# Four channel blocks of K transposed by DMA instead of TensorE, and a G table loaded without its zeros

## The chip, the cores and the metric

The kernel runs on one core of a Trainium2 chip. The metric is the device time of one execution in microseconds (us), the median over several runs. The core has five engines with instruction streams of their own: TensorE (PE in the profile, its weight loads PEld), VectorE (DVE), ScalarE (ACT), GpSimd (POOL) and SyncE (SP). SP computes nothing here; its queue issues nearly all DMA transfers, in order.

## The reference

The function is one layer on a sequence of 2048 positions with 640 channels: a convolution block and a dense block, each with a residual sum. All tensors are bf16.

```python
x = A_q
k_shift = sum(k_pad[:, t:t + S, :] * shift_k[:, ks - 1 - t] for t in range(4))   # causal, 4 taps per channel
kv = k_shift * v
y = irfft(rfft(kv padded to 2S) * rfft(ssm_k padded to 2S))[:S] + kv * ssm_D    # long convolution per channel
h = x + layernorm(x) * y
act = mish(layernorm(h) @ w1 + b1)
out = h + act @ w2                                                              # w1 640x1728, w2 1728x640
```

## The kernel before

**Data.** The 640 channels are five blocks of 128 (block m, or b). The 2048 positions are 128 partitions times 16 positions. Short names stand for the steps:

- d_n0 to d_n4, d_k0 to d_k3, d_v0, d_v1, d_x0 to d_x2, d_g0 to d_g7, d_w1, d_w2, d_t2m: loads of ssm_k (N), K, V, the input, the table G, the weights and another table.
- k1pe / k1ev: TensorE transposes of N (L635) into PSUM, and the copies ("evictions") from PSUM to SBUF on ACT (L428) or DVE (L430).
- ktpe / ktev: the same for K (L590). Each block has two halves, x and y, of eight 128x128 transposes each. ktsh (L601, POOL) then makes a copy of one half that is shifted by one column; it serves the part of the four-tap filter that reaches across the boundary.
- cfpe, coef, wsh (L502, L516): the filter's coefficients, spread into small weight matrices, ten products on POOL.
- kspe / kv: the filter as matmuls (L609, L610) and its product with V, which also empties PSUM (L613, DVE).
- s1k, s1v: the first step of the long Fourier transform, of N and of K times V (L561, L562), with evictions. The last letters of a name give its block and part.
- s2k, s2v: the second step, with table G as weights (L662 for N in 22 groups of six frequencies, L697 for K times V), with evictions.
- sw: DMA transfers that swap neighbouring partitions of the transformed N (L678, L679). p1, p2: the products in the frequency domain (L716, L720), on DVE and POOL.
- i1 (L756, L757) and i2 (L813): the inverse transform. y are its evictions, wb and h the sums, bn, pow, hc the second layer norm.
- trd: DMA transposes of the normalised tiles (L849) for most of the positions; trpe does the first two on TensorE.
- m1pe, hb: the first dense matmul (L910) and Mish on ACT (L915). m2q, m2pe, res: the second dense matmul (L931, L943) and the residual sum (L948). d_out: the stores.

**Buffers.** Large SBUF tiles are used several times. `ra` holds K, later K times V, later a table; `rb` holds V and, before that in its first part, the transposed N of block 2, so d_v0 waits until s1kpe of block 2 has read it. `rn` holds N, later swapped spectra, later w2. `uv` holds the transposed K and the wsh matrices before it holds the spectrum of K times V. `xb` holds the other wsh matrices before part of the input. PSUM is a ring of eight banks of 512 fp32 columns.

**Order.** A list of words such as `ktev1y:a` fixes for each step its engine (t PE, a ACT, v DVE, p POOL, d SP's DMA queue, s ACT's DMA queue) and its place among that engine's steps. `_schedule` turns it into a program with planned durations, by which slots and the order of issue are chosen. On the chip every engine takes its steps in that order, and waits on semaphores where a step needs another's result.

Of the kernel before, what the change touches and what calls it, by code (L numbers as in the profile page):

```python
# [12 lines left out]
BF16 = mybir.dt.bfloat16  # L13
# [3 lines left out]
S = 2048  # L17
D = 640
FF = 1728
FP = 1792  # L20
P = 128
# [5 lines left out]
d_id:s wz:v d_dr:s d_sk:s d_go:d wm:t d_n0:d d_n2:d d_n3:d d_x0:d d_n1:d d_n4:d d_k2:d dcpe:t warm:a dcev:v dq0:v k1pe0y:t k1pe0x:t k1pe2y:t d_k3:d  # L27
k1ev0y:v d_k1:d dq2:v k1pe2x:t k1ev0x:v k1ev2y:v k1ev2x:a s1kpe0_0x:t s1kev0_0x:v d_k0:d s1kpe0_3x:t s1kpe0_1y:t s1kpe0_2x:t s1kpe0_2y:t s1kpe2_2x:t
s1kpe2_3x:t s1kpe2_0y:t s1kev0_3x:a ln1_2:v s1kev0_2y:a s1kev0_2x:a dq1:v cfpe:t kz:p ln1p2:p s1kev2_3x:a dq3:v s1kev2_2x:a ln1_3:v s1kev0_1y:v dq4:v
d_g4:d k1pe3y:t k1ev3y:a coef:a d_v1:d wsh4_0:p ln1p3:p k1pe1x:t d_g3:d d_g2:d k1ev1x:a wsh2_1:p wsh0_0:p wsh4_1:p wsh1_1:p wsh3_1:p wsh2_0:p d_g1:d  # L30
k1pe1y:t k1pe3x:t k1ev1y:v k1pe4y:t k1pe4x:t k1ev3x:v k1ev4x:v s1kpe1_0y:t s1kpe2_2y:t s1kpe1_1y:t wsh1_0:p s1kev2_2y:a s1kpe2_1y:t k1ev4y:v
s1kpe3_0x:t s1kev1_0y:a s1kev2_0y:a s1kpe2_1x:t s1kpe1_1x:t s1kpe0_3y:t s1kev0_3y:a s1kev3_0x:v s1kev1_1x:v s1kpe4_0x:t s1kev4_0x:v s1kpe4_3y:t
s1kev4_3y:a s1kpe4_3x:t s1kpe2_0x:t s1kev2_1x:a s1kpe3_2y:t s1kpe4_2x:t ln1_0:v s1kev4_3x:v s1kev3_2y:v s1kev2_1y:a s1kpe0_1x:t s1kpe2_3y:t
s1kev1_1y:v ktpe2y:t s1kev4_2x:a ktev2y:v ktpe1y:t ktpe3y:t ktpe4y:t ktpe0x:t ktpe4x:t ktev1y:a ln1_1:v d_v0:d ktpe0y:t ktev3y:a s1kev2_0x:v ktev4x:v
ktev4y:v s1kev2_3y:a s1kev0_1x:a ktev0y:a ktpe3x:t ktpe2x:t s1kpe3_3y:t s1kpe3_2x:t s1kev3_3y:v s1kpe4_0y:t s1kpe4_1y:t s1kpe4_1x:t s1kev4_1y:a
s1kev3_2x:a s1kpe3_3x:t s1kpe1_3y:t ktev0x:v s1kpe0_0y:t ktev3x:v kspe3_1y:t s1kpe1_0x:t ktev2x:a s1kev1_3y:a s1kev4_0y:a ktpe1x:t s1kpe3_1y:t d_g0:d
s1kev1_0x:a s1kev0_0y:a s1kev3_1y:a s1kpe3_1x:t ktsh4:p wsh0_1:p s1kev4_1x:v ktsh1:p wsh3_0:p ktsh2:p ktsh0:p ln1p1:p ktsh3:p s1kev3_3x:v kv3_1y:v
s1kpe4_2y:t s1kpe1_2y:t ktev1x:v s1kev4_2y:a s1kev3_1x:v s1kpe1_2x:t d_small:p s1kpe3_0y:t s1kev1_2y:v s1kpe1_3x:t kspe0_1x:t kspe1_1x:t s1kev3_0y:v
# [957 lines left out]
```

## Time and profile before

| What | Value |
|---|---|
| Median of three runs | 221.71 us (221.61 to 222.79) |
| Profiled execution, first to last instruction (its own time; the profile gives no other) | 219.6 us |
| PE busy | 212.6 us, 97% |
| DVE busy | 145.1 us, 66% |
| ACT busy | 133.1 us, 61% |
| POOL busy | 75.6 us, 34% |
| DMA moved | 31.03 MB |

A row of a group reads: line, engine, operation, output <- inputs, shape and count; then total busy us and mean ns; then the idle time before these instructions and what ended it. The rows of 40 slices give the busy share of each slice in tenths, 5.49 us a slice. Matmul durations overlap in time, so their spacing, not their mean duration, says what they cost. The clock granted to TensorE was 1.000 throughout.

### The profile page before, as it was taken

What the parts mean: (1) busy time and instruction counts of PE and PEld (TensorE: products, weight loads), DVE (VectorE), ACT (ScalarE), POOL (GpSimd) and SP (SyncE); (2) the same over time, 40 slices, a digit from 0 to 9 for tenths busy, and PEclk for the clock granted to TensorE, in tenths of its full rate; (3) what the DMA queues carried; (4) which work ended last, traced back from release to release, by engine and by line L of the source; (5) the groups of instructions that cost most, each with busy time, mean ns of one, the idle gap of its engine ahead of it and who ended that gap; (6) DMA issues with size and microseconds to landing.
All of it is one profiled execution on the core that took longest, in us unless ns stands there. A gap on an engine that the chain in (4) does not pass through costs nothing.

```text
span 219.6 us, 6285 instructions
## 1 busy us (share of the span) xinstructions
PE 212.6 (97%) x2611; PEld 157.8 (72%) x2618; DVE 145.1 (66%) x324; ACT 133.1 (61%) x265; POOL 75.6 (34%) x112
## 2 busy tenths in 40 slices
PE   8999999999989999999999999999999999999993
PEld 2899889999879999899876644566554444656672
DVE  0799999999999999989699889883210000213023
ACT  2488899999999999997881178600036475300000
POOL 0079997089844007124883371411000000000000
PEclk9999999999999999999999999999999999999999
DMA  6999993417999906996004401552720000000113
GB/s 213 375 419 414 412 403 130 98 23 174 192 263 285 380 10 217 325 359 105 0 0 64 91 14 45 50 103 60 86 79 19 0 3 0 0 0 3 54 60 125
DMA packets 32876, 31.03 MB, mean 141 GB/s; under 512 B 19024, under 2 KB 29264, under 8 KB 32464
## 3 DMA queue, kind: packets, MB, share of 16 engines
q1 hardware_dynamic: 32384, 30.43, 46.3%
q8 instruction: 20, 0.33, 0.7%
q10 hardware_dynamic: 368, 0.20, 0.4%
q14 instruction: 8, 0.07, 0.1%
q0 software_dynamic: 96, 0.00, 0.0%
HBM read 20.47 MB, written 2.62 MB: 105 GB/s over the span
## 4 chain that ended last, share of the span: by engine, by line
PE 76%; ACT 11%; DVE 5%; issue 3%; SPq 2%; DMA 1%; DVEq 0%; ACTq 0%
PE ps L943 26%; PE ps L910 26%; ACT uk L428 8%; PE ps L813 4%; ACT uv L428 3%; PE ps L756 3%; PE ps L757 3%; PE ps L635 2%; PE ps L561 2%; PE ps L473 2%; PE ps L590 2%; DMA xa<-uk 1%; DVE ra L613 1%; PE ps L931 1%; DVE uv L716 1%
## 5 line engine op out<-in xcount | busy, mean ns | idle before, releaser
L910 PE MATMUL ps<-G 128*128 128x512 bf16 (+1 forms) x319 | 58.5, 336 | 0.3
L943 PE MATMUL ps<-rn,uv 128*128 128x320 bf16 (+2 forms) x415 | 58.5, 299 | 0.1
L915 ACT ACTIVATE uv<-ps,b1s 128x512 bf16<-128x512 f32 (+1 forms) x65 | 35.6, 607 | 36.6 <-PE ps L910 34.8
L943 PEld LDWEIGHTS <-uv 128*128 128x128 bf16 x416 | 39.2, 98 | 18.5 <-issue 1.6
L910 PEld LDWEIGHTS <-G 128*128 128x128 bf16 x325 | 31.1, 98 | 24.0 <-issue 0.9
L428 ACT CAST uk<-ps 128x512 bf16<-128x512 f32 (+1 forms) x91 | 47.2, 703 | 1.9 <-PE ps L562 1.4
L948 DVE TENSOR_TENSOR xb<-ps,xb 128x320 bf16<-128x320 f32 (+2 forms) x12 | 5.6, 488 | 42.6 <-ACT uv L915 24.3
L428 ACT CAST uv<-ps 128x512 bf16<-128x512 f32 (+2 forms) x54 | 28.6, 766 | 0.0
L430 DVE CAST uk<-ps 128x512 bf16<-128x512 f32 (+2 forms) x32 | 20.1, 661 | 0.6 <-ACT uk L428 0.5
L756 PE MATMUL ps<-a,uv 128*128 128x128 bf16 x160 | 18.7, 219 | 0.4 <-DVE uv L716 0.3
L756 PEld LDWEIGHTS <-uv 128*128 128x128 bf16 x160 | 17.8, 114 | 0.9 <-DVE uv L716 0.5
L837 POOL TENSOR_TENSOR r<-ve,mhalf 128x1 f32<-128x1 f32 x16 | 9.7, 613 | 25.0 <-DVE ve L834 24.9
L430 DVE CAST uv<-ps 128x512 bf16<-128x512 f32 (+2 forms) x28 | 17.2, 669 | 0.2 <-ACT uv L428 0.2
L948 DVE TENSOR_TENSOR xa<-ps,xa 128x320 bf16<-128x320 f32 x12 | 5.6, 486 | 14.0 <-PE ps L943 13.9
L613 DVE TENSOR_TENSOR ra<-ps,rb 128x512 bf16<-128x512 f32 x20 | 12.9, 683 | 0.3 <-ACT uv L428 0.3
L720 POOL TENSOR_TENSOR rn<-rn,uv 128x1024 bf16<-128x1024 bf16 x5 | 10.6, 2127 | 7.2 <-PE ps L697 7.2
L697 PE MATMUL ps<-uv,G 128*128 128x64 bf16 (+1 forms) x256 | 12.2, 197 | 0.8 <-ACT uv L428 0.6
L662 PE MATMUL ps<-uk,G 128*128 128x160 bf16 x128 | 12.4, 230 | 0.3 <-ACT uk L428 0.2
L697 PEld LDWEIGHTS <-G 128*128 128x128 bf16 x256 | 10.8, 96 | 1.4 <-issue 1.0
L428 ACT CAST rb<-ps 128x512 bf16<-128x512 f32 (+1 forms) x30 | 11.3, 464 | 0.7 <-PE ps L813 0.4
L561 PE MATMUL ps<-cst,ra 128*64 128x128 bf16 x160 | 10.7, 219 | 0.4
L562 PE MATMUL ps<-cst,ra 128*64 128x128 bf16 x160 | 10.9, 222 | 0.0
(111 smaller groups left out, 375.7 us busy)
## 6 DMA issues: line engine op xcount, KB each, us to landing
G<-tab_g SPq DMA_DIRECT2D x8, 512.0 KB, 14.1
rn<-in_A_ssm_k_dram SPq DMA_DIRECT2D x5, 512.0 KB, 6.3
ra<-in_A_k_dram SPq DMA_DIRECT2D x4, 640.0 KB, 11.4
rb<-in_A_v_dram SPq DMA_DIRECT2D x2, 1280.0 KB, 13.9
G<-in_B_w_dram SPq DMA_DIRECT2D x5, 432.0 KB, 7.3
rn<-in_B_w_dram SPq DMA_DIRECT2D x1, 2080.0 KB, 13.4
rn<-uk SPq DMA_DIRECT2D x8, 256.0 KB, 4.3
rb<-uk SPq DMA_DIRECT2D x8, 256.0 KB, 4.5
```

Source lines behind the costliest of these rows:

```text
L428: nc.scalar.copy(o, i)
L430: nc.vector.tensor_copy(o, i)
L561: nc.tensor.matmul(ps[0:64, k, :], lhs, mc, start=True, stop=True)
L562: nc.tensor.matmul(ps[64:128, k, :], lhs, ms, start=True, stop=True)
L613: nc.vector.tensor_tensor(kv_w[:, m, k:32:2, 8 * h:8 * h + 8, :], ps.rearrange("p (l t d) -> p d t l", l=4, t=8), raw_v[:, 8 * h:8 * h + 8 ...
L662: nc.tensor.matmul(ps[:, o:o + 160], g_v[:, f, :], KA[:, :, f, :], start=True, stop=True)
L697: nc.tensor.matmul(ps[:, fl * n:fl * n + n], g_v[:, f0 + h * kf + fl, :], VX[x][:, :, f0 + h * kf + fl, :], start=True, stop=True)
L756: nc.tensor.matmul(pz[:, k, :], V[c.i][:, dg // 4, :, dg % 4], a12[:, 0, :], start=True, stop=False)
L910: nc.tensor.matmul(ph[:, 0:w], w1[:, dc, fc * P:fc * P + P], lnhT_of(u)[:, dc, 0:w], start=(dc == 0), stop=(dc == NDC - 1))
L915: nc.scalar.activation(hb_of(u)[:, fc, 0:w], rt.tile[:, 0:w], ACT.Mish, bias=b1s[:, fc:fc + 1], scale=1.0)
L943: nc.tensor.matmul(po[:, 0:d1 - d0], hb_of(u)[:, fc, tl * P:(tl + 1) * P], w2[:, fc, d0:d1], start=False, stop=(fc == NFC - 2))
L948: nc.vector.tensor_tensor(x, rt.tile[:, 0:d1 - d0], x, ALU.add)
```

## The change

**K.** For blocks 1 to 4 (`KX`) the transposes on TensorE and their evictions are gone. In their place POOL copies K with its elements reordered into a buffer (kp, eight steps of 1024 elements per partition), and a DMA transpose from SP's queue (kx, eight steps of eight 128x128 blocks) writes the transposed half. Block 0 stays as it was. The buffers lie in xb, hc and the end of N's region in rn; the last four wait until N's transposes have read it.

**Shifted copies.** The two halves now lie side by side, 16 columns behind the start of a row of 272, with column 15 zeroed. The shifted half is read as a window that starts one column earlier, so ktsh is gone. Both wsh matrices of a block now lie in uv, and xb is free of them.

**G.** Three quarters of G are zeros. G is now zeroed on chip (gz: four steps, one on DVE, three on POOL), and only its nonzero blocks are loaded: eight transfers of 32 partitions with pieces of 256 bytes. To keep the pieces together, the four frequencies of a group lie interleaved, so a matmul reads its weights with a step of four elements. The rows that G produces change their order, and the table a12 of the inverse transform is permuted to match. A load of G now serves 64 frequencies, four loads each.

**Order.** All of the order list is new. Among its differences: most s2k steps come before the filter (kspe), the loads of G follow K, the first seven kx stand behind d_v0 and the last behind sw0_1, and d_w2 stands behind trd2 and trd3. Several evictions and products change their engine.

```diff
+k1ev1y:a k1ev0y:v dq1:v k1ev0x:v k1pe1x:t s1kpe0_1x:t s1kpe0_3x:t s1kpe0_3y:t s1kpe0_2x:t k1ev1x:v s1kev0_1x:v s1kpe1_1y:t s1kpe1_2x:t s1kpe1_0x:t
...
+ln1_2:v k1pe4x:t s1kev0_2x:a k1ev3y:a k1ev3x:a s1kev1_0x:a k1ev4y:a coef:a wsh3_0:p wsh0_0:p wsh4_0:p d_k0:d d_k1:d wsh0_1:p wsh1_1:p wsh1_0:p kp1_0:p
+d_k2:d d_k3:d kp3_1:p kp1_1:p kp2_0:p d_g7:d d_g0:d s1kpe1_3x:t s1kpe3_0y:t s1kpe2_2x:t s1kpe1_3y:t k1ev4x:v s1kpe3_2y:t s1kpe2_3y:t s1kpe2_3x:t
...
+s2kpe_8x:t d_v1:d d_v0:d kx1_1:d kx1_0:d kx3_0:d kx2_0:d kx2_1:d s2kpe_9x:t kx3_1:d s2kpe_1y:t kx4_0:d ktev0y:v ktev0x:v s2kev_4y:a s2kev_7x:a
...
+s2kev_19y:a s2kev_16x:a s2kpe_2x:t kspe1_1x:t sw0_1:d kx4_1:d s2kev_13x:a s2kev_2x:a kv1_1x:v kspe1_0x:t kspe1_0y:t kspe1_1y:t s1vpe0_1y:t s1vpe0_3x:t
...
+hb0_1:a hb0_5:a m1pe0_6:t m1pe0_2:t i2pc7:t i2pc6:t i2pc8:t y15b:a y10b:a y8b:a trd2:d hb0_2:a trd3:d d_w2:d m1pe0_11:t y7b:v i2pc12:t i2pc5:t ln1_4:v
...
-    T["g"] = np.moveaxis(G, 4, 6).reshape(128, 128 * 128)
+    full = np.moveaxis(G, 4, 6).transpose(5, 0, 1, 2, 3, 4, 6)
+    T["g"] = np.stack([full[d, :, :, d].reshape(32, 32, 4, 32).swapaxes(2, 3).reshape(32, 128 * 32) for d in range(4)])
...
-    g_v = gt[:].rearrange("p (f q) -> p f q", q=P)
+    g_v = gt[:].rearrange("p (b q f) -> p b f q", q=P, f=4)
...
-    kt_s = [t[:, 0:3072].rearrange("p (g a t) -> p g a t", g=8, a=3) for t in at_uv]
-    wsh = [[x.rearrange("p (l n) -> p l n", l=4) for x in (t[:, 3072:3776], xb[:, 704 * m:704 * m + 704])] for m, t in enumerate(at_uv)]
+    kt_s = [t[:, 0:2176].rearrange("p (g n) -> p g n", n=272) for t in at_uv]
+    wsh = [[t[:, 2176 + 704 * k:2880 + 704 * k].rearrange("p (l n) -> p l n", l=4) for k in range(2)] for t in at_uv]
+    KX = [1, 2, 3, 4]
+    KP = dict(zip([(m, h) for h in (1, 0) for m in KX], [xb[:, 0:1024], xb[:, 1024:2048], xb[:, 2048:3072], hc_t[:, 0:1024], *(rn[:, 4096 + 1024 * i:5120 + 1024 * i] for i in range(6))]))
...
-        return lambda: nc.sync.dma_start(gt[:, i * 2048:(i + 1) * 2048], dram["g"][:, i * 2048:(i + 1) * 2048])
+        d, h = i % 4, i // 4
+        return lambda: nc.sync.dma_start(gt[d:P:4, h * 8192:h * 8192 + 8192].rearrange("p (b q) -> p b q", q=512)[:, :, 128 * d:128 * d + 128], dram["g"][d, :, h * 2048:h * 2048 + 2048].rearrange("p (b q) -> p b q", q=128))
+    c_gz = [OP(f"gz{i}", [("dve", 1.77), ("pool", 3.5)], emit=(lambda e, i=i: (nc.vector if e == "dve" else nc.gpsimd).memset(gt[:, i * 4096:(i + 1) * 4096], 0.0))) for i in range(4)]
...
+        for h in (1, 0):
+            def kpf(e, b=b, h=h):
+                src = raw_k[:, h * 8 * D:(h + 1) * 8 * D].rearrange("p (n k r) -> p k r n", k=2, r=20)[:, :, 4 * b:4 * b + 4, :]
+                o = KP[b, h].rearrange("p (k r n) -> p k r n", k=2, r=4)
...
+            kp = OP(f"kp{b}_{h}", [("pool", 1.3), ("dve", 1.15), ("act", 1.0)], d_k[2 * h:2 * h + 2], emit=kpf)
+            k_free[h].append(kp)
+
+            def kxf(e, b=b, h=h):
+                nc.sync.dma_start_transpose(kt_s[b][:, :, 144 - 128 * h:272 - 128 * h], KP[b, h])
+            kt_done[b, h] = OP(f"kx{b}_{h}", ("dma", 1.55), [kp], emit=kxf, lat=3.2)
...
-                    nc.tensor.matmul(o, t[:, q, h, :], w[:, 0:128], start=True, stop=False)
-                    nc.tensor.matmul(o[:, 0:48], t[:, q, 0 if h else 2, :], w[:, 128:176], start=False, stop=True)
+                    nc.tensor.matmul(o, t[:, q, 144 - 128 * h:272 - 128 * h], w[:, 0:128], start=True, stop=False)
+                    nc.tensor.matmul(o[:, 0:48], t[:, q, 144:272] if h else t[:, q, 15:143], w[:, 128:176], start=False, stop=True)
...
-    d_g = [DMA(f"d_g{i}", 0.525e6, emit_g(i), deps=d_n[:1], prio=0.6, lat=4.9) for i in range(8)]
+    d_g = [DMA(f"d_g{i}", 0.35e6, emit_g(i), deps=d_n[:1] + c_gz[i // 4 * 2:i // 4 * 2 + 2], prio=0.6, lat=4.5) for i in range(8)]
```

182 lines of the change are left out of this document (89 added, 93 removed).

## The prediction

> **What bounds the kernel now.** I read the page from the top: busy totals, then the span in slices.
>
> ```profile
> span 219.6 us, 6285 instructions
> PE 212.6 (97%) x2611; PEld 157.8 (72%) x2618; DVE 145.1 (66%) x324; ACT 133.1 (61%) x265; POOL 75.6 (34%) x112
> DVE  0799999999999999989699889883210000213023
> ACT  2488899999999999997881178600036475300000
> DMA  6999993417999906996004401552720000000113
> ```
>
> PE at 97% says little, because overlapping matmuls are each counted in full. DVE and ACT tell more: both are nearly always busy from about 25 us to about 85 us and idle for long stretches later. Four stretches of the windows view show the change of bound. Its columns are stretch and length, then busy time (instructions) of PE, PEld, DVE, ACT and POOL, clock, DMA share and GB/s.
>
> ```profile
> 5.00:25.00 20.00, 19.88 (x419) 18.13 (x418) 17.65 (x40) 14.56 (x24) 12.51 (x14) 1.00 1.02 403
> 25.00:66.00 41.00, 39.20 (x910) 36.27 (x905) 40.50 (x69) 40.50 (x86) 28.84 (x27) 1.00 0.69 197
> 66.00:87.00 21.00, 20.55 (x365) 19.95 (x362) 20.52 (x32) 21.00 (x45) 6.15 (x7) 1.00 0.65 216
> 87.00:219.60 132.60, 128.94 (x925) 81.95 (x929) 66.33 (x184) 55.55 (x112) 27.62 (x56) 1.00 0.29 71
> ```
>
> From 5 to 25 us the DMA engines are full (1.02) and PE has a queue of work. From 25 to 66 us ACT and DVE each work 40.5 of 41 us: copying PSUM into SBUF sets the pace. From 87 us PE alone is the limit. The chain of waits agrees: in the first stretch it runs through the K transposes (L590), afterwards through ACT.
>
> ```profile
> 18.42 4.60 PE ps L590 x72
> 25.93 1.36 ACT uk L428 x3
> 31.39 2.88 ACT uk L428 x6
> ```
>
> **The change part by part.** The sum is made against the profiled span of 219.6 us. The median of the three runs is 221.71 us, 2.1 us more; I carry these 2.1 us unchanged.
>
> *Evictions of K.* Block 0 keeps its transposes (L590); blocks 1 to 4 lose theirs and the eight evictions behind them. Groups by line give the number of evictions, merged timeline rows their real spacing.
>
> ```profile
> L428 ACT COPY uv<-ps 128x1024 bf16<-128x1024 bf16 x4 | 4.0, 1030 | 0.7 <-PE ps L590 0.7
> L430 DVE COPY uv<-ps 128x1024 bf16<-128x1024 bf16 x6 | 3.9, 680 | 0.0
> 19.60 1.93 ACT L428 COPY uv<-ps 128x1024 bf16<-128x1024 bf16 x2 [0.74 <-PE ps L590]
> 22.32 1.28 DVE L430 COPY uv<-ps 128x1024 bf16<-128x1024 bf16 x2
> 25.93 4.05 ACT L428 CAST uk<-ps 128x512 bf16<-128x512 f32 x8
> 54.89 3.67 DVE L430 CAST uv<-ps 128x512 bf16<-128x512 f32 x6
> 60.52 1.28 DVE L720 TENSOR_TENSOR rn<-rn,uv 128x1024 bf16<-128x1024 bf16 x2
> ```
>
> A 1024 copy costs 1.93/2 = 0.97 us on ACT and 0.64 on DVE; a 512 cast 0.51 on ACT and 0.61 on DVE; a product 0.64 on DVE. ACT loses four K evictions (3.9 us), DVE four of six (2.6); two stay on DVE. The new order also moves work, by counting its words. ACT gains one 1024 copy, two s1v and four s2v casts and loses three s2k casts: +0.97 + 3 x 0.51 = +2.5, net -1.4. DVE loses what ACT gains and takes three s2k casts back: -0.64 - 3 x 0.61 = -2.5. It also gets three products from POOL, +1.9. Its net is -3.2. Evictions can be handed from one engine to the other, so I take the mean of the two, **-2.3 us**. The lower end of the gain is ACT's 1.4 alone.
>
> *Transposes of K on PE.* 64 of the 80 go, 64 x 4.60/72 = 4.1 us. They sit in the DMA-bound stretch and delay the evictions, not the end; 4.1 us is the upper end of the gain if nothing takes their place. Their weight-load time also prices the table read below.
>
> *Reading table G with a step of four elements.* The 384 weight loads of L662 and L697 become strided. The products' loads at L756 already have that step, L590 a step of 40.
>
> ```profile
> L697 PEld LDWEIGHTS <-G 128*128 128x128 bf16 x256 | 10.8, 96 | 1.4 <-issue 1.0 <-DVE uv L430 0.2
> L756 PEld LDWEIGHTS <-uv 128*128 128x128 bf16 x160 | 17.8, 114 | 0.9 <-DVE uv L716 0.5 <-issue 0.3
> L590 PEld LDWEIGHTS <-ra 128*128 128x128 bf16 x80 | 5.2, 147 | 0.2
> 41.63 0.31 PE ps L697 x8
> 76.32 0.06 PE ps L757
> ```
>
> A load grows from 96 to about 114 ns, and such loads keep 55 to 60 ns spacing at L757. For the 128 matmuls of L662 (160 columns) that hides. The 256 of L697 now come every 0.31/8 = 39 ns: between 0 and 256 x (57 - 39) = +4.6 us. L590's 51 ns longer load costs only 64 - 55 = 9 ns of spacing, so a load 18 ns longer should cost about 3: 0.8 us of PE time. It lies where ACT and DVE work 40.5 of 41 us: taken as 0. Without that cover it is 0.8.
>
> *Zeros and the load of G.* One quarter of G is zeroed on DVE, three on POOL. DVE waits 5.2 us for its first input and POOL 10.2 us.
>
> ```profile
> DVE d_col L488 <- PE ps L486: 5.2, 1, 5.2
> POOL ve L791 <- DVE mv L787: 10.2, 1, 10.2
> 13.28 1.37 POOL L516 TENSOR_TENSOR uv<-cst,coef 128x704 bf16<-128x704 bf16 x1 [0.78 <-ACT coef L428]
> L467 DVE MEMSET hc<- 128x64 uint32 x1 | 0.1, 112 | 0.8 <-PEq L980 0.8
> L601 POOL COPY uv<-uv 128x1016 bf16<-128x1016 bf16 x5 | 5.1, 1029 | 0.0
> ```
>
> On DVE 2048 words at 112/64 ns or less are at most 3.6 us: hidden. On POOL, 4096 elements at the copy's 1.0 ns are 4.1 us, so three end near 13 us, where the first coefficient product starts now (13.28): 0, and 4 us later at worst for POOL. G shrinks from 4.2 to 1.05 MB in 256-byte pieces; the swap transfers (L678), mostly short packets, show the rate of such pieces.
>
> ```profile
> G<-tab_g SPq DMA_DIRECT2D x8, 512.0 KB, 14.1
> DMA packets 7103, 2.08 MB, mean 189 GB/s; under 512 B 6077, under 2 KB 7101, under 8 KB 7101
> ```
>
> N, x0, K and V are 8.5 MB at the 403 GB/s above, 21 us; G at 189 GB/s takes 5.5 us instead of 10.4. Counted from 2.5 us the loads end near 29 us; in the page's DMA row they fill the engines to slice 5, 33 us. That opens room for the transposes and shortens nothing by itself: 0.
>
> *K's new route.* Eight permutes on POOL (taken at 1.3 us, between the 1.03 of the copy and 2.13 of a two-input product) replace five shift copies; eight DMA transposes follow on SP's queue.
>
> ```profile
> L516 POOL TENSOR_TENSOR xb<-cst,coef 128x704 bf16<-128x704 bf16 x5 | 6.8, 1366 | 0.0
> L720 POOL TENSOR_TENSOR rn<-rn,uv 128x1024 bf16<-128x1024 bf16 x5 | 10.6, 2127 | 7.2 <-PE ps L697 7.2
> L786 DVE BATCH_NORM_STATS2 st<-x 128x6 f32<-128x320 bf16 x8 | 3.5, 482 | 0.7 <-DMA x<-in_A_q_dram 0.7
> G<-hc SPq DMA_TRANSPOSE x14, 2.7
> 121.94 1.21 SPq L849 DMA_TRANSPOSE G<-hc  x1
> ```
>
> Coefficients near 16 us (13.3 now; in the new order more evictions stand before them), six wsh products (8.2), eight permutes and small work put the last permute near 36 us on POOL. On SP the transposes stand behind d_v0, which waits until PE has read block 2 of N: 38 s1k casts at some 0.56 us, ten copies of N at some 0.8 and the statistics' 3.5 are 33 us on two engines from about 8 us, so about 25 to 26 us. A transpose here has 8 blocks against 5 at L849: 8/5 x 1.21 = 1.9 us spacing. Seven are issued by 40 us and landed by 43; sw0_1 and the last follow, landed near 47. Meanwhile PE and the eviction engines have 36 of 43 s2k pieces (18 us of casts, 9 us on two engines) and block 0: kspe1 is wanted near 37 us, kspe2 near 44, kspe4 near 50. Their transposes land near 31, 39 and 47. Cost 0, with 3 to 6 us of margin; past that each microsecond is exposed. The end of the margin is reached at a spacing near 3 us.
>
> The Trainium skill, "VectorE: DVE Perf Modes", section on the three transpose paths, speaks against this: it lists 1309 ns for a 128x128 block through the DMA against 390 ns on TensorE and advises TensorE where PSUM will do. By that figure, an estimate, a transpose of 8 blocks would be 10.5 us and the sum some 50 us worse. The trace disagrees: 5 blocks land 2.7 us after issue, so the page's figure cannot be a rate.
>
> *The rest.* The shift copy's removal frees 5.1 us of POOL, off the path. Past 66 us PE does the same matmuls. One order change matters: w2's load moves behind the transposes trd2 and trd3.
>
> ```profile
> 98.33 17.66 SPq L849 DMA_TRANSPOSE G<-hc  x3
> rn<-in_B_w_dram SPq DMA_DIRECT2D x1, 2080.0 KB, 13.4
> 110.11 0.38 PE ps L931 x4
> 87.73 0.39 SPq L769 DMA_DIRECT2D rn<-in_B_w_dram  x1
> ```
>
> It used to go out at 87.7. Now it goes about 98.3 - 2.3 + 2 x 1.2 = 98.4. Its first reader (L931, m2q0) comes at 110.1 - 2.3 + two 256-wide groups moved ahead of it (1.1) = 108.9. The 13.4 us to landing included other loads' backlog; at 403 GB/s and 2 us it would be 7.6. So it lands between 106.0 and 111.8: between 0 and 2.9 us of stall. I take 0.
>
> **Sum**: -2.3 in evictions, the rest covered: 219.6 - 2.3 = 217.3 us of span, 219.4 us as a median.
>
> **The rivals.**
> 1. *Transposes late (slower).* If SP lets one land before the next starts, the spacing is 8/5 x 2.7 = 4.3 us. kx2 and kx3 then end at 26 + 6 x 4.3 = 52 where they are wanted at 44 to 46; some 2 us of s2v work remain to fill in. 6 us are exposed: 219.4 + 6 = 225.4. For it speaks that traffic of V and the swaps surrounds them; against it, the 1.21 us spacing at L849. It decides above about 4 us of spacing, where the exposed time exceeds the 2.3 gained.
> 2. *POOL late (slower).* Permutes at 2.13 and zeros at 5.7 us each (1.4 ns per element): 5 + 8 x 0.83 = 12 us later, kspe2 near 51, exposed 5: 224.4. Against it: the plain copy's 1.03.
> 3. *w2 late (same).* Stall 2.9 at L931: 219.4 + 2.9 = 222.3.
> 4. *No relief (same).* ACT is relieved by 1.4 only, and strided loads cost 0.8 on PE: 221.1.
> 5. *All of PE's 4.1 us gained (faster).* If the L590 row of the chain is what delays the evictions: 217.6.
>
> **How the numbers follow.** Half a per cent, 1.1 us, is what a measurement of this kernel tells from no change. Chances: forecast 0.45, rival 5 0.16, rival 4 0.08, rival 3 0.09, rival 1 0.15, rival 2 0.07. The forecast and rival 5 are faster, 0.61; rivals 3 and 4 same, some of 3 slower: 0.13; slower 0.26. The range goes from 217.0 to 224.4, leaving out rival 1's tail; the forecast's own is 218.0 to 220.4 (gains of 1.4 to 3.7).
>
> **What would show it.** Right: sixteen matmuls on L590; ACT and DVE full until about 2 us earlier; no PE wait on the transposed tile (uv) or on w2 (rn); the first product on POOL near 13 to 17 us; transposes about 2 us apart. Wrong: PE waits for uv longer than 1 us between 35 and 52 us, or SP holding a transpose behind d_v0 past 30 us; L697's loads far above 114 ns; or ACT and DVE idle in that stretch while G or V is on its way.

## The result and the profile after

The changed kernel takes 227.55 us (median; 227.36 to 229.41) where the kernel before takes 221.76: a ratio of 1.027, 95% interval 1.024 to 1.031. It is slower by 5.8 us; the forecast was 2.3 us faster. The profiled span grew by 6.0 us, from 219.6 to 225.6. Here and below, ratios leave out an execution that is over 1.5% above the fastest of its kernel, while medians keep it.

The page of the changed kernel, its busy totals and the span in 40 slices of 5.64 us:

```profile
span 225.6 us, 6184 instructions
PE 212.0 (94%) x2554; PEld 156.3 (69%) x2554; DVE 146.6 (65%) x325; ACT 128.7 (57%) x255; POOL 97.9 (43%) x122
...
DVE  3789896974999999998979899868200210101141
ACT  2599997983999999899760054750453025420000
POOL 9939999987494600624884565223000000000000
PEclk9999999997999999999999999999999999999999
```

Counted from 1, POOL is busy without a break from slice 4 to slice 8, where it had idle time before; ACT and DVE have holes in slices 7, 9 and 10, and the clock dips in slice 10. The windows view gives the stages (stretch, length, busy time of PE, PEld, DVE, ACT, POOL with instruction counts, clock, DMA share, GB/s):

```profile
5.00:25.00 20.00, 18.89 (x422) 16.33 (x421) 17.27 (x39) 15.96 (x29) 15.97 (x9) 1.00 1.00 335
25.00:66.00 41.00, 34.23 (x749) 32.05 (x747) 33.57 (x56) 34.09 (x72) 35.25 (x37) 0.96 0.93 191
```

Most of the loss lies between 25 and 66 us. ACT and DVE were busy there for 40.5 of 41 us each; now they are busy for 34. PE idles 41 - 34.2 = 6.8 us instead of 41 - 39.2 = 1.8, that is 5.0 us more. The chain of waits names the place (start, length, what; engine, tile and line):

```profile
23.17 2.24 POOL rn L610
25.41 4.51 POOL xb L610 x2
29.91 6.75 POOL rn L610 x3
...
36.72 0.21 POOL uv L532 x5
36.92 2.22 POOL xb L610
39.14 2.25 POOL hc L610
...
42.74 3.98 POOL uv L518 x3
...
48.34 5.64 DMA uv<-hc
...
54.03 0.22 PE ps L624
```

L610 are the permutes (kp), L532 the zeroing of column 15 (kz), L518 the wsh products, L615 the DMA transposes (kx), L623 and L624 the filter's matmuls. Where ACT stood in the chain before, POOL stands now. The groups by line give the prices of a zeroing step (L545) and of a permute (L610, the four that write to rn):

```profile
L545 POOL MEMSET G<- 128x4096 bf16 x3 | 10.4, 3512 | 0.3 <-POOLq L996 0.3
L610 POOL COPY rn<-ra 128x1024 bf16<-128x1024 bf16 x4 | 9.1, 2304 | 0.0
```

A permute takes 2.30 us. Eight of them end at 41.4 us instead of near 36. What waits for them, by the view of waits between 25 and 66 us (engine, tile, line, releaser: us, times, longest):

```profile
PE ps L624 <- DMA uv<-hc: 2.6, 1, 2.6
PE ps L624 <- POOL uv L532: 1.5, 1, 1.5
PE ps L623 <- POOL uv L518: 1.2, 1, 1.2
...
DVE ra L627 <- POOL rn L610: 2.1, 1, 2.1
```

Four different things stand behind the permutes: the last transposes, the zeroed column, the remaining wsh products, and the product kv (L627, DVE), which writes into `ra` and so must wait until the permutes have read K there. SP's queue shows how the last transpose comes so late:

```profile
31.52 5.54 SPq L615 DMA_TRANSPOSE uv<-rn  x3
...
46.93 0.65 SPq L694 DMA_DIRECT2D rn<-uk  x1
47.62 0.66 SPq L695 DMA_DIRECT2D rn<-uk  x1
48.34 1.77 SPq L615 DMA_TRANSPOSE uv<-hc  x1
```

Its permute ends at 41.4 us, but in the queue it stands behind the two transfers of the swap sw0_1, which could not go before 46.9 us; it is issued at 48.3 and PE goes on at 54.0. The swap itself was held by a transpose, by the waits of SP's queue:

```profile
SPq L694 <- DMA uv<-rn: 3.2, 1, 3.2
```

The swap writes into `rn`, where four of the permuted pieces of K lie until their transposes have read them. So the new route also delays the swaps. The stretch in which PE waits, in windows of one microsecond:

```profile
52.00:53.00 1.00, 0.00 (x0) 0.00 (x0) 0.00 (x0) 0.64 (x2) 0.00 (x0) 1.00 0.26 51
53.00:54.00 1.00, 0.00 (x0) 0.00 (x0) 0.00 (x0) 0.00 (x0) 0.86 (x1) 0.76 1.29 278
54.00:55.00 1.00, 0.97 (x16) 0.98 (x17) 0.20 (x1) 0.00 (x0) 1.00 (x1) 0.50 1.35 217
55.00:56.00 1.00, 1.00 (x20) 1.00 (x18) 0.75 (x2) 0.00 (x0) 1.00 (x2) 0.50 1.35 218
56.00:57.00 1.00, 1.00 (x18) 1.00 (x16) 0.61 (x2) 0.83 (x2) 1.00 (x1) 0.54 1.35 217
57.00:58.00 1.00, 1.00 (x37) 0.93 (x36) 1.00 (x2) 0.66 (x2) 0.83 (x3) 1.00 1.35 220
```

While PE waits, its granted clock falls to a half, and it stays there until 57 us: 16 to 20 matmuls per microsecond, and 37 in the next (not all of the same size). At 0.50, 0.50 and 0.54 the lost clock is 0.50 + 0.50 + 0.46 = 1.46 us, an estimate of what it costs.

### The profile page after: what moved, and what is told of

Same layout as the page of the kernel before. It is cut to its first block, busy times and chain, and to the rows that moved or that the text cites. A ratio compares the mean times of both kernels' runs of the same rounds, so it can differ in the third digit from the quotient of the medians.

```text
span 225.6 us, 6184 instructions
## 1 busy us (share of the span) xinstructions
PE 212.0 (94%) x2554; PEld 156.3 (69%) x2554; DVE 146.6 (65%) x325; ACT 128.7 (57%) x255; POOL 97.9 (43%) x122
## 4 chain that ended last, share of the span: by engine, by line
PE 54%; POOL 19%; ACT 10%; DVE 8%; issue 4%; DMA 3%; POOLq 0%; ACTq 0%; DVEq 0%
PE ps L959 19%; PE ps L926 17%; ACT uv L430 6%; POOL uv L518 5%; PE ps L772 4%; POOL rn L610 4%; PE ps L773 4%; POOL xb L610 3%; ACT rb L430 3%; DMA uv<-hc 3%; PE ps L475 2%; POOL ra L818 2%; PE ps L649 2%; DVE st L802 2%; POOL r L808 2%
## 5 line engine op out<-in xcount | busy, mean ns | idle before, releaser
L430 ACT CAST uk<-ps 128x512 bf16<-128x512 f32 (+1 forms) x88 | 44.3, 661 | 3.0 <-PE ps L678 1.5
L430 ACT CAST uv<-ps 128x512 bf16<-128x512 f32 (+2 forms) x60 | 30.0, 672 | 4.9 <-PE ps L713 3.5
L432 DVE CAST uk<-ps 128x512 bf16<-128x512 f32 (+1 forms) x35 | 21.6, 668 | 0.9 <-issue 0.5
L627 DVE TENSOR_TENSOR ra<-ps,rb 128x512 bf16<-128x512 f32 x20 | 12.6, 685 | 6.7 <-PE ps L624 3.4
L518 POOL TENSOR_TENSOR uv<-cst,coef 128x704 bf16<-128x704 bf16 x10 | 13.4, 1368 | 4.0 <-ACT coef L430 4.0
L713 PE MATMUL ps<-uv,G 128*128 128x64 bf16 (+1 forms) x256 | 13.2, 204 | 1.0 <-DVE uv L432 0.8
L432 DVE CAST uv<-ps 128x512 bf16<-128x512 f32 (+2 forms) x22 | 13.3, 666 | 0.4 <-ACT uv L430 0.2
L713 PEld LDWEIGHTS <-G 128*128 128x128 bf16 x256 | 11.7, 116 | 1.7 <-DVE uv L432 0.9
L624 PE MATMUL ps<-uv 128*128 128x48 bf16 x80 | 8.7, 194 | 4.2 <-DMA uv<-hc 2.6
L816 ACT ACTIVATE ra<-xb,nmr,r 128x640 bf16<-128x640 bf16 x4 | 3.6, 916 | 15.9 <-POOL nmr L809 15.9
L732 DVE TENSOR_TENSOR uv<-uv,uk 128x1024 bf16<-128x1024 bf16 (+1 forms) x15 | 10.9, 755 | 0.6 <-POOL rn L736 0.6
L678 PE MATMUL ps<-uk,G 128*128 128x160 bf16 x128 | 10.8, 232 | 0.5 <-ACT uk L430 0.4
```

What stands on the lines that cost most here:

```text
L430: nc.scalar.copy(o, i)
L432: nc.vector.tensor_copy(o, i)
L518: (nc.gpsimd if e == "pool" else nc.vector).tensor_tensor(out, a, b, ALU.mult)
L627: nc.vector.tensor_tensor(kv_w[:, m, k:32:2, 8 * h:8 * h + 8, :], ps.rearrange("p (l t d) -> p d t l", l=4, t=8), raw_v[:, 8 * h:8 * h + 8 ...
L713: nc.tensor.matmul(ps[:, fl * n:fl * n + n], g_v[:, (f0 + h * kf + fl) // 4, (f0 + h * kf + fl) % 4, :], VX[x][:, :, f0 + h * kf + fl, :], ...
L732: eng.tensor_tensor(v, v, K[c.i][:, b0:b1, f0:f1, :], ALU.mult)
```

## The experiments

The theory after the first comparison (P): the permutes are the cause, at 2.30 instead of 1.3 us. The rivals: the order of queues around them (Q), the other parts of the change, and a forecast gain that was never there. Times stand beside 221.7 to 221.9 us of the kernel before, run on the same chip. The changed kernel's 227.55 us comes from its own four runs alone, so experiments are compared with it through the kernel before.

### The price of a permute

**e1: the same copies, read contiguously.**

```diff
-src = raw_k[:, h * 8 * D:(h + 1) * 8 * D].rearrange("p (n k r) -> p k r n", k=2, r=20)[:, :, 4 * b:4 * b + 4, :]
-o = KP[b, h].rearrange("p (k r n) -> p k r n", k=2, r=4)
+src = raw_k[:, h * 8 * D + 1024 * b:h * 8 * D + 1024 * b + 1024]
+o = KP[b, h]
```

> The changed kernel, but the eight permutes on POOL read 1024 neighbouring elements of K instead of elements 40 apart; the filter then works on the wrong elements of K, so this part of the layer is not computed, while every other step keeps its size. Theory P (the permutes' 2.30 us each, against 1.0 us for a plain copy, delay everything that stands behind them on POOL): a permute falls to 1.0 to 1.1 us, the last one ends about 10 us sooner, PE's idle time between 25 and 66 us falls from 6.8 to about 2 us, the clock stays at 1.0, and the time falls to 218 to 221 us. Theory Q (SP's queue: the transposes themselves, and the last one behind a swap transfer): the last transpose still lands near 52 to 54 us, and the time stays within 1.5 us of 227.5. Theory S (POOL is slow because DVE and POOL disturb each other): permutes stay above 1.8 us.

Measured 223.41 us, ratio 1.007 (1.004 to 1.010): 4.1 us of the 5.8 are gone. That is between the two ranges: theory P's 218 to 221 was too low, theory Q's 226 to 229 too high, and S fell. One group of e1:

```profile
L610 POOL COPY rn<-ra 128x1024 bf16<-128x1024 bf16 x4 | 4.0, 1033 | 0.0
```

and the stage by windows:

```profile
25.00:66.00 41.00, 36.79 (x835) 34.65 (x830) 37.06 (x63) 38.02 (x81) 27.33 (x37) 1.00 1.12 217
```

So the same number of elements, written to the same places, costs 1.03 us read in a row and 2.30 us read with a step of 40 elements (80 bytes). PE's idle time falls from 6.8 to 4.2 us, not to the 2 that P expected, and the clock stays whole in this profiled execution. In four of e1's ten executions the mean granted clock was 0.991 or 0.992, like the 0.992 of the changed kernel's profiled execution. The six at 0.997 or above took 221.69 to 224.48 us, these four 223.19 to 226.22. And the kernel is still not faster than before.

**e7: the loops exchanged**, four neighbours read, written with a step of 128.

```diff
-src = raw_k[:, h * 8 * D:(h + 1) * 8 * D].rearrange("p (n k r) -> p k r n", k=2, r=20)[:, :, 4 * b:4 * b + 4, :]
-o = KP[b, h].rearrange("p (k r n) -> p k r n", k=2, r=4)
+src = raw_k[:, h * 8 * D:(h + 1) * 8 * D].rearrange("p (n k r) -> p k n r", k=2, r=20)[:, :, :, 4 * b:4 * b + 4]
+o = KP[b, h].rearrange("p (k r n) -> p k n r", k=2, r=4)
```

> The changed kernel with the permutes' two inner loops exchanged: four neighbouring elements are read, and written 128 elements apart. Same bytes, same result. If POOL's time follows the step of what it reads, a permute falls to 1.0 to 1.5 us and the time to 222 to 225 us. If it follows the number of access-pattern dimensions or any step that isn't one, a permute stays at 2.2 to 3 us and the time at 227 us or above.

Measured 244.87 us, ratio 1.104, from two executions. Both expectations for the permute fell:

```profile
L610 POOL COPY rn<-ra 128x1024 bf16<-128x1024 bf16 x4 | 19.0, 4973 | 0.0
```

Reading runs of four and writing with a step costs 5.0 us, more than reading with a step and writing in a row. Which of the two makes it, the short runs or the step of the writes, this run doesn't tell. Either way this reordering of 1024 elements on POOL costs two to five times a copy.

**e6: the permutes shared out**, four on POOL, two each on ACT and DVE, with kz first and the last transpose ahead of the swap.

```diff
-d_k2:d d_k3:d kp3_1:p kp1_1:p kp2_0:p d_g7:d
+d_k2:d d_k3:d kp2_0:p d_g7:d
...
-s1kev3_3x:a kp3_0:p
+s1kev3_3x:a kp3_1:a kp3_0:p
...
-kz:p s1kpe3_1x:t kp2_1:p kp4_1:p s1kev3_1x:a s1kev4_2y:v s1kev4_0x:a
+s1kpe3_1x:t s1kev3_1x:a s1kev4_2y:v kp1_1:v s1kev4_0x:a
...
-s1kev2_0y:a ln1_0:v
+s1kev2_0y:a kp2_1:a ln1_0:v
...
-ln1_1:v s1kev0_0y:v
+ln1_1:v kp4_1:v s1kev0_0y:v
```

> The changed kernel with four of the eight permutes on ACT and DVE (two each), the other four on POOL, and kz and the last transpose ahead. All of the layer is computed. Theory P: POOL's chain is 9.2 us shorter, less the wait for coefficients nothing is added there, the last permute ends near 33 us; two permutes on ACT and DVE cost these engines about 1 to 1.5 us each, that is 2 to 3 us per engine in a stretch where they have idle time: 221 to 224 us. Theory Q (rate of the transposes): 224 to 226 us. Below 220.5 us it would beat the kernel before.

Measured 226.69 us, 1.023 (1.020 to 1.025), above both ranges. The same permute on ACT and DVE:

```profile
L608 ACT COPY xb<-ra 128x1024 bf16<-128x1024 bf16 x2 | 4.7, 2334 | 0.9 <-DMA ra<-in_A_k_dram 0.9
L610 DVE COPY xb<-ra 128x1024 bf16<-128x1024 bf16 x1 | 2.0, 2020 | 0.6 <-DMA ra<-in_A_k_dram 0.6
```

They cost 2.33 and 2.0 us there (the second one on DVE 1.7), on the engines that set the pace; besides, they wait for K in front of evictions that PE needs. The windows show what follows:

```profile
20.00:22.00 2.00, 0.00 (x0) 0.00 (x0) 2.00 (x2) 2.00 (x1) 2.00 (x2) 1.00 0.49 98
...
28.00:32.00 4.00, 4.00 (x65) 3.66 (x63) 2.36 (x4) 3.34 (x7) 4.00 (x2) 0.50 0.37 89
```

PE idles some 2.9 us from 20 us on, and its clock is at a half until about 32.5 us.

### The rest of the change, alone

**e8: the table G alone** on the kernel before (zeroed on chip, loaded without its zeros, read with a step; K as before). **e3: G and the windows** instead of shifted copies, all five blocks on TensorE.

```diff
-nc.tensor.matmul(ps[:, o:o + 160], g_v[:, f, :], KA[:, :, f, :], start=True, stop=True)
+nc.tensor.matmul(ps[:, o:o + 160], g_v[:, f // 4, f % 4, :], KA[:, :, f, :], start=True, stop=True)
...
-nc.gpsimd.tensor_copy(t[:, :, 2, 1:128], t[:, :, 1, 0:127])
```

> The kernel before with only table G loaded without its zeros. The pair of parts (table and windows) was slower by 0.33%. If the table makes that (strided weight loads: 384 loads of 113 ns against 96), the time is again 222.2 to 222.8 us. If the windows make it (a window that starts 30 bytes into a row), the table alone stays within 0.15% of the kernel before, 221.4 to 222.0 us.

> The kernel before with two of the change's three parts: table G loaded without its zeros (four zeroing steps, weights read with a step of four elements) and the shifted copies of K replaced by windows. All five blocks of K stay on TensorE. Theory P and theory Q both hold that these parts cost nothing: 220.5 to 222.5 us. Theory G (the strided weight loads, 113 ns against 96, and the short packets cost time): 223.5 us or more.

Measured 222.11 us (1.002, 1.000 to 1.003) for e8 and 222.64 (1.003, 1.002 to 1.005) for e3: 0.3 us, and 0.7 (by the ratio) to 0.95 (by the medians) with both. e8 lies between its two ranges, e3 just above its first; whether table or windows cost more is not settled. The larger group of weight loads in e3:

```profile
L698 PEld LDWEIGHTS <-G 128*128 128x128 bf16 x256 | 11.7, 115 | 1.1 <-issue 0.7
```

It grew from 96 ns to 115, where 114 was forecast, and the whole table costs 0.3 us. These parts don't explain the loss.

### The queues and the clock

**e2: kz ahead of everything on POOL, the last transpose ahead of the swap.**

```diff
-gz1:p gz3:p dcev:v
+gz1:p gz3:p kz:p dcev:v
...
-kz:p s1kpe3_1x:t kp2_1:p
+s1kpe3_1x:t kp2_1:p
...
-sw0_1:d kx4_1:d
+kx4_1:d sw0_1:d
```

> The changed kernel with two words of the order moved: the zeroed columns of the shifted window (kz) go ahead of the permutes on POOL, and the last transpose goes ahead of the first swap transfer on SP. Theory Q: the two waits that these words cause (1.5 us for the zeroed column, up to 2.8 us for the last transpose) go, and with them part of the clock loss: 223 to 225 us. Theory P: the last permute still ends at 41 us and the products for blocks 2 and 4 still stand behind it, so that waits for those take their place: 225.5 to 227.5 us.

**e4: PE kept busy** while it waits, with twelve matmuls on zeros before the first kspe4 step.

```diff
-p2_0_3:p p2_0_2:p kspe4_0x:t
+p2_0_3:p p2_0_2:p fill:t kspe4_0x:t
+for _ in range(12):
+    nc.tensor.matmul(ps[:, 0:512], wz, wz4, start=True, stop=True)
```

> The changed kernel with twelve matmuls on zeros (some 2.6 us) put on PE just ahead of the filter of block 4, where PE idles. If the granted clock falls because PE is idle, it stays at 1.0 from 54 to 58 us, and the time falls by 1 to 1.5 us, to about 226.2. If the clock does not follow PE's idling, or its fall is covered, the time stays at 227.5 us, or rises by up to 1 us where the matmuls delay the filter.

e2 measured 226.51 us (225.99 without one execution of 230.39), 1.019 (1.014 to 1.024): in P's range, and these two words of the order are worth 1.0 to 1.6 us. The waits for the column and for the last transpose are gone, but PE waits for casts of DVE instead,

```profile
PE ps L565 <- DVE uv L432: 2.2, 2, 2.1
```

and the clock falls to 0.50 behind that wait. e4 measured 226.10, 1.019 (1.016 to 1.021), 1.45 us less than the changed kernel, and the clock no longer falls in its windows:

```profile
52.00:53.00 1.00, 1.00 (x6) 0.49 (x5) 0.10 (x1) 0.82 (x2) 0.00 (x0) 1.00 0.44 23
...
54.00:56.00 2.00, 1.57 (x40) 1.41 (x39) 0.86 (x2) 0.06 (x1) 2.00 (x2) 1.00 1.33 233
```

The mean clock was 0.999 or 1.000 in all four executions of e4 and 0.983 to 0.992 in all four of the changed kernel. Work that computes nothing makes the kernel faster: the fall of the clock follows the idling of PE, and its price agrees with the 1.46 us estimated above. The Trainium skill, "TensorE: Matmul & The Clock Gate", Part 1, states two levels, full and a half, and a fall after an idle window of about 3.4 us. The levels agree with the 1.00 and 0.50 here; the length doesn't, as a wait of 2.6 us was enough in the changed kernel.

**e5: e1 and e2 together.** **e11: e5 with five DVE products (p1, p2) moved behind the casts.** **e12: e2 with the same move.**

```diff
-s1vpe4_0x:t p1_0_3:v p2_0_7:v p1_0_2:v s1vev2_3x:a
+s1vpe4_0x:t s1vev2_3x:a
...
-s1vpe2_1x:t p2_0_6:v s1vev2_1y:a
+s1vpe2_1x:t s1vev2_1y:a
-s1vev2_0x:a p2_0_1:v s1vev4_2y:v
+s1vev2_0x:a s1vev4_2y:v
...
-s1vev3_1x:v s1vev3_2y:v
+s1vev3_1x:v s1vev3_2y:v p1_0_3:v p2_0_7:v p1_0_2:v p2_0_6:v p2_0_1:v
```

> Both edits together: the permutes read neighbouring elements (so the filter works on the wrong elements of K), and kz and the last transpose go ahead. If the permutes' length and the last transpose's place behind the swap are separate causes, the 2.0 us wait for the last transpose that the first alone still had goes too: 220.5 to 222 us, the level of the kernel before. If the transposes' own rate on the queue is what is left (three took 9.5 us there), the time stays at 222.5 to 224.

> The kernel of both edits (permutes that read neighbouring elements, so that the filter works on the wrong elements of K; kz and the last transpose ahead) with five DVE products (p1_0_3, p2_0_7, p1_0_2, p2_0_6, p2_0_1) moved behind the casts of s1v. There PE waited 2.0 us for casts behind these products, and the clock fell to 0.50 for 7 us. If that wait and the clock were what kept it at 224.4 us, the clock stays at 1.0 and the time is 220 to 222 us. If the rest is elsewhere, 223 to 225 us.

> The changed kernel with kz and the last transpose ahead and the same five products moved behind the casts; the permutes keep their 2.30 us and all of the layer is computed. Theory P: what remains is the permutes' delay, about 4 us over the kernel with cheap permutes: 224 to 226 us. If the order behind the permutes was the larger cause, 221 to 223 us.

Measured 224.40 us (1.012, 1.010 to 1.014), 227.07 (1.022, 1.018 to 1.026) and 228.33 (1.027, 1.024 to 1.030). All three lie above both of their ranges. In e5 PE no longer waits for a transpose; a DVE product that took 2.60 us at 53.2 stood ahead of casts instead, by its waits

```profile
PE ps L565 <- DVE uv L432: 2.0, 1, 2.0
```

and the clock fell later, and for longer (to 65 us):

```profile
57.00:58.00 1.00, 0.00 (x0) 0.00 (x0) 1.00 (x3) 1.00 (x3) 1.00 (x1) 1.00 0.90 226
...
59.00:62.00 3.00, 3.00 (x53) 2.68 (x53) 3.00 (x6) 1.07 (x2) 3.00 (x3) 0.50 1.03 231
```

Moving those products away turned the wait into another one (L713 waiting 3.3 us for a cast of DVE, in e11 and e12 alike). Orders mended by hand at one place opened a gap at the next; e1's 223.41 stayed the best of these. e1's profiled execution waited 1.9 us for its last transpose without a fall of the clock, e5's 2.0 us with one, and e1's own executions differ in their clock. What decides it was not settled.

### Fewer blocks

**e9: block 4 alone, e10: blocks 2 and 4**, by the new route in the order of before (K's other blocks on TensorE, windows, table G as before).

```diff
-wsh2_0:p d_g1:d
+wsh2_0:p kp4_1:p kp4_0:p d_g1:d
...
-d_g7:d d_g5:d
+d_g7:d d_g5:d kx4_1:d kx4_0:d
...
+KX = [4]
```

> The kernel before, its order, table and nine of ten transposed pieces as they were, with the new route for block 4 of K alone (two permutes on POOL in the place of the shift copies, two DMA transposes on SP's idle stretch near 25 us) and the windows in place of all shift copies. Theory P (the route costs nothing as long as POOL has room): two permutes of 2.3 us replace five shift copies of 1.03, PE loses 16 transposes (1.0 us) and DVE two evictions (1.2 us): 220.6 to 221.7 us. If the route costs in itself (transposes beside V's load, a wait for a DMA instead of a copy), 222.5 us or more.

> The same with blocks 2 and 4 on the new route: four permutes, 9.2 us on POOL against 5.1 for the shift copies, which must end before the first product of K and V can overwrite K (26.5 us in the kernel before). Theory P: POOL's chain is 4 us longer than in the kernel before, the first products wait, and the time lies at 221 to 223.5 us, above that of one block. If POOL had room for four, it is below the one-block kernel: 220 to 221 us.

Measured 222.92 us (1.004, 1.003 to 1.006) and 227.77 (1.026, 1.023 to 1.028). e9 went against theory P: one block, with room on POOL, is 1.0 us slower, the case in which the route costs in itself (the windows, which e9 has too, can be part of it). e10 lies 4 us above its range: two blocks in this order cost as much as four in the new one. e10's waits:

```profile
DVE ra L631 <- POOL xb L605: 4.4, 2, 3.0
...
PE ps L627 <- POOL uv L518: 3.1, 1, 3.1
```

Here the products that overwrite K come early, and they wait 4.4 us for the permutes: the dependency through `ra`. PE waits 3.1 us for a wsh product that stands behind the permutes.

### The route taken apart

Cheap permutes and better orders all ended above the kernel before. So was the forecast gain there at all, and what does each half of the route cost? Four runs answer it.

e13, plain loads in the place of the transposes and no permutes (e14 keeps the eight kp):

```diff
-d_k2:d d_k3:d kp3_1:p kp1_1:p kp2_0:p d_g7:d
+d_k2:d d_k3:d d_g7:d
...
-nc.sync.dma_start_transpose(kt_s[b][:, :, 144 - 128 * h:272 - 128 * h], KP[b, h])
+nc.sync.dma_start(kt_s[b][:, :, 144 - 128 * h:272 - 128 * h], A_k.rearrange("b (p a) d -> p (b a d)", a=NT)[:, h * 5120 + 1024 * b:h * 5120 + 1024 * b + 1024].rearrange("p (g n) -> p g n", n=128))
```

e15, transposes of one contiguous copy (e16 has the last of them ahead of the swap, as e2):

```diff
+if b == KX[0]:
+    kp = OP("kp1_0", [("pool", 1.3)], d_k[0:2], emit=lambda e: nc.gpsimd.tensor_copy(KP[1, 1], raw_k[:, 0:1024]))
...
-nc.sync.dma_start_transpose(kt_s[b][:, :, 144 - 128 * h:272 - 128 * h], KP[b, h])
+nc.sync.dma_start_transpose(kt_s[b][:, :, 144 - 128 * h:272 - 128 * h], KP[1, 1])
```

> The eight permutes are left out, and the eight DMA transposes become plain loads of 256 KB of K from DRAM at the same places of the queue; the transposed K is not formed, so the filter works on other elements. This keeps everything else of the change: evictions and TensorE transposes gone, table G read with a step, the new order. If the forecast's relief of 2.3 us is there once K's route costs nothing: about 219.5 us (218.5 to 220.5) beside 221.7 of the kernel before. If table and windows cost the 0.9 us that they cost alone and the order hides the rest of the relief: 221 to 222. If something besides the route of K slows the changed kernel: above 223.5.

> As e13, but with the eight permutes back on POOL, at 2.3 us each; their results are used by nothing, while the product that overwrites K still waits for them. If the permutes delay through POOL alone (the zeroed column, the filter's weights and the overwriting of K queue behind them): 3 us or more above e13, about 225 to 226.5. If they delay through the transposes that wait for them: within 1 us of e13, and the difference to the changed kernel's 227.5 lies in the transposes.

> The changed kernel with its eight DMA transposes, but with one contiguous copy of 1024 elements of K on POOL instead of the eight permutes; all eight transposes read that one copy, so the filter works on other elements. It completes the four combinations: neither (e13, 220.2), permutes alone (e14, 224.0), transposes alone (this one), both (the changed kernel, 227.5). If the transposes cost little by themselves and only their lateness behind the slow permutes counts: within 1 us of e13, about 220 to 221. If they hold up the queue and the other transfers by themselves, and the two costs add: 3 us above e13, about 223 to 224.

> As e15, with the last transpose ahead of the swap sw0_1 in SP's queue instead of behind it. If what e15 costs above e13 is the last transpose held behind the swap: within 0.7 us of e13. If the transposes' own transfers cost it: no better than e15.

| | no permutes | eight permutes |
|---|---|---|
| plain loads | e13: 220.19 us, 0.992 (0.988 to 0.995) | e14: 223.97 us, 1.009 (1.005 to 1.012) |
| DMA transposes | e15: 221.86 us, 0.999 (0.996 to 1.001) | changed kernel: 227.55 us, 1.027 (1.024 to 1.031) |

e16 measured 221.45 us, 0.997 (0.994 to 1.001). The stage from 25 to 66 us in e13, by windows:

```profile
25.00:66.00 41.00, 38.98 (x870) 36.72 (x869) 39.90 (x67) 40.49 (x86) 22.31 (x25) 1.00 0.95 241
```

in e14:

```profile
25.00:66.00 41.00, 37.13 (x833) 34.77 (x834) 38.04 (x63) 38.39 (x80) 38.78 (x38) 1.00 0.88 226
```

and in e15:

```profile
25.00:66.00 41.00, 37.94 (x856) 35.66 (x851) 38.40 (x65) 39.30 (x84) 21.60 (x24) 1.00 1.08 224
```

e13 lies in the range of the forecast's relief. e14 is more than 3 us above e13, the case of a delay through POOL alone, though it is 1 us below the time named for it. e15 and e16 lie between their ranges. With the route out of the way ACT and DVE are full again, PE idles 2.0 us, and the kernel is 1.6 us faster than before (the traffic of the plain loads is in that time). The permutes alone, whose results nobody reads, cost 223.97 - 220.19 = 3.8 us: through POOL's queue and the overwriting of K, with no transpose behind them. e14's waits name the same three (zeroed column, wsh product, K), beside one of 1.2 us on PE for which the profile shows no releaser:

```profile
PE ps L623 <- POOL uv L518: 1.2, 1, 1.2
...
PE ps L624 <- POOL uv L532: 0.6, 1, 0.6
...
DVE ra L627 <- POOL rn L610: 1.2, 1, 1.2
```

The transposes alone, in the place of plain loads, cost 1.7 us. The place behind the swap is some 0.4 of that (e16), which the overlapping intervals don't tell from nothing, and PE waits 1.2 us for a transpose in both. In SP's queue of e15 (start, length) they wait for no permute:

```profile
24.66 17.80 SPq L608 DMA_TRANSPOSE uv<-xb  x7
```

Seven take 17.80 us, 2.54 each on average, but single ones 1.3 to 5.2. That is not a price of the transposes alone: e13's seven plain loads take 13.38 us at the same place of the queue, right behind the loads of G and V, and in the changed kernel, where they are issued later, a transpose takes 1.2 to 1.8 us.

Both costs together make 220.19 + 3.8 + 1.7 = 225.7; the changed kernel takes 227.55. The missing 1.9 us exist only where both meet. The clock stays at 1.00 in this stage in the profiled executions of e13, e14 and e15 and falls in the changed kernel's, where the longest wait is 2.6 us and e4's gain was 1.45 us. (By the mean clock, one of e14's four executions, three of e15's ten and all four of the changed kernel had such a fall.) Of the four, only the changed kernel has a swap that waits for late transposes out of `rn`, too; how the 1.9 us divide is not shown.

No version that computes the whole layer beat the kernel before; the nearest is e8 at 222.11 us.

## Why the prediction was wrong

**The step that failed** is "Cost 0, with 3 to 6 us of margin" for "K's new route", and first in it the price of the permutes: "taken at 1.3 us, between the 1.03 of the copy and 2.13 of a two-input product". Neither row bounds it. Both are operations that read runs of neighbouring elements; the permute reads with a step of 40 elements, and costs 2.30 us, above both ends. The rows had a warning: weight loads with that same step (L590) took 147 ns against 96. The Trainium skill, "GPSIMD Engine Reference", section on performance pitfalls, states for custom code on POOL that reads with a step above 8 bytes cost half as much again; if that held for the built-in copy, 1.03 would become 1.5 us, an estimate. The direction agrees with the trace, the size doesn't: 2.30 / 1.03 = 2.2.

The price is not the whole of it. With permutes at 1.03 us, below the 1.3 taken, e1 still takes 223.41 us, 4.0 above the forecast; with one such copy in the place of eight, e15 takes 221.86, 2.5 above it; e13, without permutes or transposes, is 0.8 above it. The margin was not there even at the price assumed.

**The second failure is who waits.** The step "kspe1 is wanted near 37 us, kspe2 near 44, kspe4 near 50" counted only the readers of the transposed K. The permutes also hold kv, which overwrites K in `ra` (2.1 us of waiting, and 4.4 in e10), the zeroed column, which stands behind six of them in POOL's list (1.5), and the last wsh products (1.2). The working named none of these, but each can be read from the order list and the buffers. e7, where a permute takes 5.0 us, makes it plain: there PE waits 16.2 us for the zeroed column. e14 shows that the permutes cost 3.8 us with no transpose behind them, so a margin counted for the transposes alone did not cover this path.

**Point by point.**
- Evictions, -2.3 us: e13, all of the change but the route's permutes and transposes, gives -1.6 us (220.19, in the range of 218.0 to 220.4 stated for the forecast). No run has the evictions alone.
- TensorE's 4.1 us from the K transposes: not gained, as taken; rival 5 falls with e13.
- Table G, 0 with 0.8 as its price uncovered: 114 to 116 ns per load as forecast, and 0.3 us in e8. Zeroing took 3.5 us a step on POOL where 4.1 was the estimate; the first wsh product began at 15.2 us, in the range named.
- SP's queue: d_v0 went out by 23.7 us, earlier than the 25 to 26 forecast, and d_v0 was never what held the transposes. It was the permutes that held them. Their spacing, taken as 1.9 us, is 1.2 to 1.8 in the changed kernel and 2.54 on average in e15, right behind the loads of V: under the 3 us at which the margin was to end, yet worth 1.7 us. The 1309 ns per block of the Trainium skill ("VectorE: DVE Perf Modes", section on the three transpose paths), which the prediction set aside, is no rate here either: 2.54 us for eight blocks is 0.32 us per block.
- The last landing, 47 us: 54.0. The permutes were 5 us late, and sw0_1, behind which the last transpose stands, waited for late transposes out of `rn`; the working had this swap right behind the seventh transpose.
- w2: PE shows no wait for it. Rival 3 did not happen.
- Rival 2 (POOL late, 0.07), the rival that was thought least likely, is what happened as far as the permutes go: 2.13 us there, 2.30 measured. Its zeros at 5.7 us took 3.5, and POOL was 5 us late, not 12. It was priced at 224.4 by 5 us of exposure; it became 227.55. The transposes' own cost and the fall of the clock are not in that price.

The clock's fall was not foreseen at all: the profile before showed 1.000 throughout, and its longest wait of PE between 18 and 70 us was 0.6 us.

## What to carry to other kernels

A price taken "between two rows" needs a row with the same access pattern; where none has it, look for any row with that step, on any engine, and put the upper end above the largest row. When work moves to an idle engine, list what stands behind it in that engine's order and who overwrites what it reads, not only who reads its result. And where TensorE has been kept busy throughout, a single wait can cost more than its length: here one of 2.6 us was followed by a fall of the clock worth some 1.45 us.

## What the runs showed that was not expected

- A copy of 128 x 1024 bf16 on POOL took 1.03 us read in a row, 2.30 read with a step of 40 elements, and 5.0 in runs of four neighbours written with a step of 128. On ACT the step-40 copy took 2.33 us, on DVE 1.7 to 2.0.
- TensorE's clock fell to 0.50 after waits of 2.0 to 2.9 us, and stayed there for some 3.3 us (changed kernel), 7 us (e5) and 10 us (e6, PE idling for part of it); after the 1.9 us of e1's profiled execution it did not fall.
- Two transposes issued while V and G were still loading kept SP's queue for 10.5 us, by e9's queue; in the changed kernel two that were issued later, one after the other, took 2.90:

```profile
25.90 10.52 SPq L610 DMA_TRANSPOSE uv<-xb  x2
```

- A DVE product of 1024 elements took 2.60 us in e5, by the timeline, and another one 0.68; POOL ran two products of its own until 55.27 us, beside the long one:

```profile
53.22 2.60 DVE L732 TENSOR_TENSOR uv<-uv,uk 128x1024 bf16<-128x1024 bf16 x1 [1.06 <-POOL rn L736]
56.34 0.68 DVE L732 TENSOR_TENSOR uv<-uv,uk 128x1024 bf16<-128x1024 bf16 x1
```

  That POOL held the long one up is likely from these times, but no run took POOL's product away alone.
